# Decode attention with a gated token mixer: the last block's K halves loaded together, its neighbours' products spread, and the last projection's weights copied to 128 columns

## The chip, the cores and the metric

The kernel runs on one core of a Trainium2 chip. The metric is the device time of one execution in microseconds; times are medians over runs. Engines: PE is TensorE (PEld its weight loads), DVE is VectorE, ACT is ScalarE, POOL is GpSimd, SP is SyncE, which here issues nearly all DMAs.

## The reference

One token attends to a cache of 65536 positions; a small token mixer and a gate stand beside it.

```python
q = (x @ wq).reshape(B, Sq, Hq, Dh)            # 16 query heads, 8 KV heads, Dh = 256, D = 448
k, v = repeat(k_cache, 2), repeat(v_cache, 2)  # k_cache, v_cache: [1, 8, 65536, 256] bf16
p = softmax(einsum(q, k) * Dh ** -0.5)
a = einsum(p, v).reshape(B, Sq, Hq * Dh) @ wo
b = mixer(layernorm(x))                        # gelu(h * w1 + b1) @ w2 + b2
g = sigmoid((x * gate_w).sum(-1))
out = g * a + (1 - g) * b                      # [1, 1, 448] bf16
```

K and V together are 537 MB, read once.

## The kernel before

**Blocks.** The cache is worked in 32 blocks (`NBLK`) of 16384 positions, four (`NB`) for each KV head. Block `n` needs 8 MB of K and 8 MB of V. Partition `p` holds 128 (`VP`) consecutive positions. K of a block lies in two tiles of 4 MB, `k_tiles[0]` and `k_tiles[1]` (kn in the profile), the first and second half of each partition's positions; V lies in one tile `vt` of 8 MB. There is one buffer of each, so a load waits until the engines have read what lies there.

**Scores.** `score_block(n)` (L348) runs over 32 steps `t`. In each, `transposes` (L321) turns four 128x128 fp32 pictures of K with the identity on PE (L325) into one of the four PSUM tiles `tps`, and DVE copies it to `kT` (L330). Two and three steps after each fourth one, `scores` (L337) multiplies the transposed K by the queries into `sc_ps` (L339). Steps 0 to 15 read `k_tiles[0]`, steps 16 to 31 `k_tiles[1]`. `hooks` is a dictionary of functions that are called after given steps, so their instructions stand at that place in each engine's order.

**Softmax and products.** `softmax(n)` (L378) takes the maximum, ACT the exponential (`p_sb`, L397) and the rescaling factor `al` of the sums so far (L402); DVE transposes the probabilities into `pT` (L405). `pv(ip)` (L362) multiplies a quarter of `pT` by a quarter of `vt` into `pv_ps`: 16 matmuls of 512 columns in four column groups (L365). `pv_block` calls it four times, and `accumulate` (L413) folds `pv_ps` into `acc` (L415). After a head's fourth block, `denominators` and `head_end` project its output with `wo_sb` and add it to `a_acc`.

**Order.** The helper `seq` keeps every engine's instructions in the order in which the program names them, SP's DMA issues too. An issue that waits holds up the issues behind it. For a usual block the order on SP is V of block n, then the two K halves of block n+1.

**The last two blocks** (`L` is block 31) are written out by hand. Block 30 issues V's first half, K of block 31 first half, V's second half, K of block 31 second half:

```python
elif n == L - 1:
    load_v(n, 0, KP)
    load_k(L, 0)
    load_v(n, KP, VP)
    load_k(L, 1)
```

Block 31's V goes into the K tiles, in six pieces of 64, 32, 16, 8, 4 and 4 positions per partition (`load_v_last`, L121), as the K rows there are read. In block 31 the hook after step 17, `before_last` (L480), does all products of block 30, `accumulate`, and `project_base` (L470), which forms `base`, the sum of the other heads' gated output and the mixer, and the gate as a column `gcol`.

**The end.** The last output is built by columns. Eight base matmuls (four of fp32, each run as two, L517) put `base` into `f_ps`, which lies in `tps[0]`. Small DVE operations make `esc`, `lsv` and, behind a matmul (L527), `rdv`. `collect` (L434) starts the sums `o_ps` from `acc`; the 256 matmuls at L538 add V of block 31, two for each of the 128 positions `j`, with V as the weights and two columns of probabilities. `oT` scales them (L545), 16 matmuls (L549) multiply by the last two heads' rows of `wo_sb`, taken as 112 columns at a stride of four, and `res` (L555) goes out (L556).

Of the kernel before, what the change touches and what calls it, by code (L numbers as in the profile page):

```python
# [8 lines left out]
FP32 = mybir.dt.float32  # L9
BF16 = mybir.dt.bfloat16  # L10
ACT = mybir.ActivationFunctionType
ALU = mybir.AluOpType
AXIS = mybir.AxisListType

HQ = 16
HKV = 8
DH = 256
REP = HQ // HKV
# [10 lines left out]
def kernel(  # L29
# [48 lines left out]
    vt = kvpool.tile([128, VP, DH], BF16, name="vt")  # L78
    kT_tiles = [work.tile([128, NJ, 128, 2], BF16, name=f"kT{i}") for i in range(2)]
    p_sb = work.tile([128, 512], BF16)  # L80
    pT = work.tile([128, 512], BF16)
    wo_sb = const.tile([128, HQ, 2, D], BF16)

    tps = [psum.tile([128, 512], FP32, name=f"tps{i}") for i in range(4)]
# [221 lines left out]
    junk = work.tile([128, REP], FP32)  # L306
    nb_tiles = [work.tile([128, 1], FP32, name=f"nb{i}") for i in range(2)]
    den = work.tile([128, 1], FP32)
    al = work.tile([128, 1], FP32)
    rden = work.tile([128, 1], FP32)  # L310
    lsv = work.tile([128, REP], FP32)
    rdv = work.tile([128, REP], FP32)
    esc = work.tile([128, 2, REP], FP32)
    oT = work.tile([128, 2, REP], BF16)
    a_acc = const.tile([1, D], FP32)
    base = const.tile([1, D], FP32)
    res = const.tile([D // NCOL, NCOL], BF16)
    gcol = const.tile([128, 1], FP32)
    state = {"t": 0}

# [38 lines left out]
        while due:  # L359
            scores(n // NB, *due.pop(0)[1])  # L360

    def pv(ip):  # L362
        for jj in range(NJ):
            grp = jj % 4
            seq(nc.tensor.matmul(  # L365
                pv_ps[32 * grp:32 * grp + 2 * REP, :, :],
                lhsT=pT[:, 32 * jj + 2 * REP * ip:32 * jj + 2 * REP * (ip + 1)],
                rhs=pairs(vt[:, 32 * ip:32 * (ip + 1), :])[:, :, jj, :],
                start=(ip == 0 and jj < 4),
                stop=(ip == NI // 2 - 1 and jj >= NJ - 4),  # L370
                tile_position=(0, 32 * grp),
            ))

    def pv_block():
        for ip in range(NI // 2):
            pv(ip)

    def softmax(n):  # L378
        b = n % NB
        nb, nb_old = nb_tiles[n % 2], nb_tiles[(n + 1) % 2]  # L380
        seq(nc.vector.tensor_reduce(out=rmax[:], in_=sc_ps[:, :], op=ALU.max, axis=AXIS.X))  # L381
        seq(nc.tensor.transpose(sm_ps[0:1, 0:128], rmax[:, 0:1], ident_f[:, :]))  # L382
        seq(nc.vector.tensor_reduce(  # L383
            out=(mrun if b == 0 else mnew)[:],
            in_=sm_ps[0:1, 0:128].rearrange("o (a i r) -> o r a i", a=4, r=REP)[:, :, :, 0:NI],
            op=ALU.max, axis=AXIS.XY,
        ))
        if b > 0:
            seq(nc.vector.tensor_tensor(out=mrun[:], in0=mrun[:], in1=mnew[:], op=ALU.max))  # L389
        seq(nc.tensor.matmul(  # L390
            sm_ps[:, 128:128 + REP], lhsT=ones_f[0:1, :], rhs=mrun[0:1, :], start=True, stop=True
        ))
        seq(nc.vector.tensor_tensor_reduce(  # L393
            out=junk[:], in0=sm_ps[:, 128:128 + REP], in1=nval[:], scale=1.0, scalar=0.0,
            op0=ALU.mult, op1=ALU.add, accum_out=nb[:, 0:1],
        ))
        seq(nc.scalar.activation(  # L397
            out=p_sb[:, :], in_=sc_ps[:, :], func=ACT.Exp, scale=scale,
            bias=nb[:, 0:1], accum_out=den[:, 0:1],
        ))  # L400
        if b > 0:
            seq(nc.scalar.activation(  # L402
                out=al[:], in_=nb_old[:], func=ACT.Exp, scale=-1.0, bias=nb[:, 0:1]
            ))
        seq(nc.vector.transpose(out=pT[:, :], in_=p_sb[:, :]))  # L405
        if b > 0:
            seq(nc.vector.scalar_tensor_tensor(  # L407
                out=lsum[:], in0=lsum[:], scalar=al[:, 0:1], in1=den[:], op0=ALU.mult, op1=ALU.add
            ))
        else:  # L410
            seq(nc.vector.tensor_copy(out=lsum[:], in_=den[:]))

    def accumulate(n):  # L413
        if n % NB > 0:
            seq(nc.vector.scalar_tensor_tensor(  # L415
                out=acc[:], in0=acc[:], scalar=al[:, 0:1], in1=pv_ps[:, :, :],
                op0=ALU.mult, op1=ALU.add,
            ))
        else:
            seq(nc.vector.tensor_copy(out=acc[:], in_=pv_ps[:, :, :]))  # L420
# [10 lines left out]

    o_ps = [hd_ps[:, 464:464 + REP], sm_ps[:, 464:464 + REP]]

    def collect(weights, stop):  # L434
        for c in range(2):
            for e in range(2):
                seq(nc.tensor.matmul(  # L437
                    o_ps[c],
                    lhsT=acc[:, e, :].rearrange("p (d c) -> p c d", c=2)[:, c, :],
                    rhs=weights[:, e, :],  # L440
                    start=(e == 0), stop=(stop and e == 1),
                ))

    def project(g):
# [6 lines left out]
                ))  # L451

    def head_end(g):
        collect(esc, True)
        for c in range(2):
            seq(nc.vector.tensor_copy(out=oT[:, c, :], in_=o_ps[c]))
        project(g)
        a_ps = hd_ps[0:1, 0:D]
        if g == 0:
            seq(nc.vector.tensor_copy(out=a_acc[:], in_=a_ps))  # L460
        else:
            seq(nc.vector.tensor_tensor(out=a_acc[:], in0=a_acc[:], in1=a_ps, op=ALU.add))
# [1 line left out]
    L = NBLK - 1  # L464

    def products(n):
        pv_block()
        accumulate(n)

    def project_base():  # L470
        seq(nc.vector.scalar_tensor_tensor(
            out=base[:], in0=a_acc[:], scalar=gate[0:1, 0:1], in1=rest[:],
            op0=ALU.mult, op1=ALU.add,
        ))
        seq(nc.tensor.matmul(
            sm_ps[:, 200:201], lhsT=ones_f[0:1, :], rhs=gate[0:1, 0:1], start=True, stop=True
        ))
        seq(nc.vector.tensor_copy(out=gcol[:], in_=sm_ps[:, 200:201]))

    def before_last():  # L480
        products(L - 1)
        project_base()

    for n in range(NBLK):
        if n == 0:
            score_block(n, {8: gate_sum, 20: mixer_tail})
        elif n < L:
            score_block(n)
        else:
            score_block(n, {17: before_last})  # L490
        if n < L - 1:
            load_v(n)
            load_k(n + 1, 0)
            load_k(n + 1, 1)
            if n == 0:
                seq(nc.sync.dma_start(
                    out=wo_sb[:], in_=A_wo.rearrange("(h p c) n -> p h c n", p=128, c=2)
                ))
        elif n == L - 1:
            load_v(n, 0, KP)  # L500
            load_k(L, 0)
            load_v(n, KP, VP)
            load_k(L, 1)
        else:
            load_v_last(L)
        softmax(n)
        if n < L - 1:
            if n % NB == NB - 1:
                denominators()
            products(n)  # L510
            if n % NB == NB - 1:
                head_end(n // NB)


    f_ps = tps[0][0:D // NCOL, 0:NCOL]
    for k in range(NCOL):
        seq(nc.tensor.matmul(  # L517
            f_ps[:, k:k + 1], lhsT=base[0:1, :].rearrange("o (m k) -> o k m", k=NCOL)[:, k, :],
            rhs=ones_f[0:1, 0:1], start=(k == 0), stop=False, skip_group_check=True,
        ))  # L520
    seq(nc.vector.tensor_scalar(
        out=esc[:], in0=fst[:], scalar1=al[:, 0:1], scalar2=None, op0=ALU.mult
    ))
    seq(nc.vector.tensor_scalar(
        out=lsv[:], in0=val[:], scalar1=lsum[:, 0:1], scalar2=None, op0=ALU.mult
    ))
    seq(nc.tensor.matmul(  # L527
        hd_ps[:, 456:456 + REP], lhsT=ones_f[:, :], rhs=lsv[:, :], start=True, stop=True
    ))
    seq(nc.vector.reciprocal(out=rdv[:], in_=hd_ps[:, 456:456 + REP]))  # L530
    seq(nc.vector.tensor_scalar(
        out=rdv[:], in0=rdv[:], scalar1=gcol[:, 0:1], scalar2=None, op0=ALU.mult
    ))
    collect(esc, False)
    for j in range(VP):
        i, jj = divmod(j, NJ)
        for c in range(2):
            seq(nc.tensor.matmul(  # L538
                o_ps[c],
                lhsT=k_tiles[j // KP][:, j % KP, :].rearrange("p (d c) -> p c d", c=2)[:, c, :],  # L540
                rhs=pT[:, 32 * jj + REP * i:32 * jj + REP * (i + 1)],
                start=False, stop=(j == VP - 1),
            ))
    for c in range(2):
        seq(nc.vector.tensor_tensor(out=oT[:, c, :], in0=o_ps[c], in1=rdv[:], op=ALU.mult))  # L545
    for c in range(2):
        for r in range(REP):
            for k in range(NCOL):
                seq(nc.tensor.matmul(  # L549
                    f_ps[:, k:k + 1],  # L550
                    lhsT=wo_sb[:, HQ - REP + r, c, :].rearrange("p (m k) -> p k m", k=NCOL)[:, k, :],
                    rhs=oT[:, c, r:r + 1],
                    start=False, stop=(r == REP - 1 and c == 1), skip_group_check=True,
                ))
    seq(nc.vector.tensor_copy(out=res[:], in_=f_ps))  # L555
    seq(nc.sync.dma_start(out=out[0, 0].rearrange("(m k) -> m k", k=NCOL), in_=res[:, :]))  # L556


# [28 lines left out]
```

## Time and profile before

| | |
|---|---|
| median of 3 runs | 1296.05 us (1295.45 to 1296.85) |
| the profiled execution, its own time | 1295.6 us |
| its span, first to last instruction | 1293.7 us |
| mean granted PE clock | 0.855 |
| HBM read | 544.22 MB, 421 GB/s over the span |
| DVE copies of K, L330 | 646.5 us busy |
| PE transposes of K, L325 | 604.9 us busy |
| chain of waits that ended last | DMA 66%, PE 31%, DVE 2% |

Stretches of the profile give busy time of each engine with the number of instructions, then the granted PE clock (1.00 is full speed), the mean busy share of the 16 DMA engines and GB/s. Timeline rows are: start in us, length in us, engine, line, operation, output and inputs, count; in brackets the engine's idle time before it and what ended it. SPq rows are DMA issues, not the transfers. Times in a trace are those of one execution.

### The profile page before, as it was taken

To read this page: it belongs to the slowest core of one execution; us is meant where nothing else is said; L and a number is where in the kernel's file an instruction comes from. 1 tells how busy PE (TensorE), PEld (TensorE's weight loads), DVE (VectorE), ACT (ScalarE), POOL (GpSimd) and SP (SyncE) were. 2 spreads that over 40 slices of the span, in tenths; PEclk is the share of its full clock that TensorE was granted. 3 is DMA by queue.
4 is the path that set the end of the run, shared out by engine and by line. 5 is a ranking of instruction groups with operands and counts; after the bars stand their busy time and mean duration, and the time that the engine had idled before them with its cause. 6 is when DMAs were issued, how large, how long until landed. Compare 5 with 4: busy or idle time off the path is not lost.

```text
span 1293.7 us, 20135 instructions
## 1 busy us (share of the span) xinstructions
PE 984.2 (76%) x8761; PEld 644.0 (50%) x8761; DVE 753.0 (58%) x1360; ACT 42.8 (3%) x107; POOL 4.2 (0%) x7
## 2 busy tenths in 40 slices
PE   5767777887777787768786678876778877777857
PEld 4445444555544555445554445554445554445536
DVE  5565555665556665556764556754556655556644
ACT  4000000000000000000000000000000000000000
POOL 1000000000000000000000000000000000000000
PEclk9887878897888988888998888987888978788877
DMA  9999999999999999999999999999999999999993
GB/s 406 426 426 432 437 425 429 434 437 436 433 426 431 433 439 435 427 434 428 431 437 434 438 424 428 436 434 432 436 429 424 439 423 442 418 427 436 392 402 134
DMA packets 17838, 545.51 MB, mean 422 GB/s; under 512 B 2260, under 2 KB 4310, under 8 KB 4822
## 3 DMA queue, kind: packets, MB, share of 16 engines
q1 hardware_dynamic: 17312, 544.22, 97.9%
q8 instruction: 68, 1.11, 0.3%
q14 instruction: 20, 0.16, 0.0%
q10 hardware_dynamic: 438, 0.01, 0.0%
HBM read 544.22 MB, written 0.00 MB: 421 GB/s over the span
## 4 chain that ended last, share of the span: by engine, by line
DMA 66%; PE 31%; DVE 2%; issue 0%; ACT 0%; ACTq 0%; DVEq 0%
DMA kn<-in_A_k_cache_dram 63%; PE tps L325 23%; PE sc_ps L339 5%; DMA vt<-in_A_v_cache_dram 3%; DVE kT L330 1%; PE pv_ps L365 1%; PE sm_ps L538 0%; PE hd_ps L538 0%; PE tps L549 0%; PE hd_ps L437 0%; ACT p_sb L397 0%; DVE pT L405 0%; PE hd_ps L448 0%; DVE rmax L381 0%; PE sm_ps L437 0%
## 5 line engine op out<-in xcount | busy, mean ns | idle before, releaser
L330 DVE COPY kT<-tps 128x1024 bf16<-128x1024 bf16 x1024 | 646.5, 684 | 185.6 <-PE tps L325 184.3
L325 PE MATMUL tps<-ident_f,kn 128*128 128x128 f32 x4096 | 604.9, 297 | 110.4 <-DMA kn<-in_A_k_cache_dram 110.4
L325 PEld LDWEIGHTS tps<-ident_f,kn 128*128 128x128 f32 x4096 | 488.0, 151 | 231.1 <-issue 115.6
L365 PE MATMUL pv_ps<-vt,pT 128*4 128x512 bf16 x1984 | 176.9, 535 | 95.2 <-DMA vt<-in_A_v_cache_dram 87.7
L339 PE MATMUL sc_ps<-kT,qpad 128*32 128x512 bf16 x2048 | 201.6, 394 | 27.7 <-DVE kT L330 27.5
L365 PEld LDWEIGHTS <-pT 128*4 128x4 bf16 x1984 | 59.0, 110 | 200.4 <-issue 140.6
L415 DVE SCALAR_TENSOR_TENSOR acc<-acc,al,pv_ps 128x512 f32<-128x512 f32 x23 | 17.2, 747 | 167.6 <-PE pv_ps L365 167.6
L339 PEld LDWEIGHTS <-qpad 128*32 128x32 bf16 x2048 | 53.0, 93 | 110.3 <-issue 101.9
L397 ACT ACTIVATE p_sb<-sc_ps,nb 128x512 bf16<-128x512 f32 x32 | 22.0, 687 | 1220.3 <-DVE nb L393 1220.3
L420 DVE COPY acc<-pv_ps 128x512 f32<-128x512 f32 x8 | 5.5, 691 | 59.0 <-PE pv_ps L365 59.0
L405 DVE STREAM_TRANSPOSE pT<-p_sb 128x512 bf16<-128x512 bf16 x32 | 22.8, 711 | 28.9 <-ACT p_sb L397 28.9
L381 DVE TENSOR_REDUCE rmax<-sc_ps 128x1 f32<-128x512 f32 x32 | 22.1, 691 | 23.2 <-PE sc_ps L339 23.2
L382 PE MATMUL sm_ps<-ident_f,rmax 128*1 128x128 f32 x32 | 8.6, 270 | 25.4 <-DVE rmax L381 25.4
L390 PE MATMUL sm_ps<-mrun,ones_f 1*128 1x2 f32 x64 | 14.4, 292 | 14.1 <-DVE mrun L389 11.7
L382 PEld LDWEIGHTS sm_ps<-ident_f,rmax 128*1 128x1 f32 x32 | 2.5, 79 | 41.5 <-DVE rmax L381 41.5
L390 PEld LDWEIGHTS sm_ps<-mrun,ones_f 1*128 1x128 f32 x64 | 11.6, 225 | 20.2 <-DVE mrun L389 16.3
L393 DVE CUSTOM_DVE_ANT_0 junk<-sm_ps,nval 128x2 f32<-128x2 f32 x32 | 5.1, 159 | 17.3 <-PE sm_ps L390 17.3
L423 PE MATMUL hd_ps<-lsum,same 128*128 128x1 f32 x14 | 3.9, 348 | 13.8 <-DVE lsum L407 13.8
L423 PEld LDWEIGHTS hd_ps<-lsum,same 128*128 128x128 f32 x14 | 3.3, 294 | 14.4 <-DVE lsum L407 14.4
L437 PE MATMUL hd_ps<-esc,acc 128*128 128x2 f32 x32 | 5.5, 275 | 6.3 <-DVE acc L415 6.0
L383 DVE TENSOR_REDUCE mnew<-sm_ps 1x2 f32<-1x64 f32 x24 | 5.1, 211 | 8.7 <-PE sm_ps L382 8.7
L437 PEld LDWEIGHTS hd_ps<-esc,acc 128*128 128x128 f32 x32 | 4.8, 212 | 9.9 <-DVE acc L415 9.6
(96 smaller groups left out, 135.3 us busy)
## 6 DMA issues: line engine op xcount, KB each, us to landing
kn<-in_A_k_cache_dram SPq DMA_DIRECT2D x63, 4096.0 KB, 26.8
vt<-in_A_v_cache_dram SPq DMA_DIRECT2D x2, 4096.0 KB
kn<-in_A_k_cache_dram SPq DMA_DIRECT2D x2, 2048.0 KB, 12.4
kn<-in_A_v_cache_dram SPq DMA_DIRECT2D x1, 4096.0 KB, 17.2
wo_sb<-in_A_wo_dram SPq DMA_DIRECT2D x1, 3584.0 KB
vt<-in_A_wq_dram SPq DMA_DIRECT2D x1, 3072.0 KB, 9.9
kn<-in_A_v_cache_dram SPq DMA_DIRECT2D x1, 2048.0 KB, 7.1
kn<-in_A_v_cache_dram SPq DMA_DIRECT2D x1, 1024.0 KB, 6.8
```

Of the source, the lines that this page charges most:

```text
L325: seq(nc.tensor.transpose(tp[:, jj * 128:(jj + 1) * 128], k_tiles[i // 4][:, i % 4 * NJ + quarter * 4 + jj, :].bitcast(FP32), ident_f[:, :],))
L330: seq(nc.vector.tensor_copy(out=kT_tiles[i % 2][:, quarter * 4:(quarter + 1) * 4, :, :].rearrange("p j n c -> p (j n c)"), in_=tp[:, :].bi ...
L339: seq(nc.tensor.matmul(sc_ps[32 * a:32 * (a + 1), :], lhsT=qpad[:, c, g, i, :], rhs=kT_tiles[i % 2][:, :, 32 * a:32 * (a + 1), c], start=( ...
L365: seq(nc.tensor.matmul(pv_ps[32 * grp:32 * grp + 2 * REP, :, :], lhsT=pT[:, 32 * jj + 2 * REP * ip:32 * jj + 2 * REP * (ip + 1)], rhs=pair ...
L381: seq(nc.vector.tensor_reduce(out=rmax[:], in_=sc_ps[:, :], op=ALU.max, axis=AXIS.X))
L382: seq(nc.tensor.transpose(sm_ps[0:1, 0:128], rmax[:, 0:1], ident_f[:, :]))
L390: seq(nc.tensor.matmul(sm_ps[:, 128:128 + REP], lhsT=ones_f[0:1, :], rhs=mrun[0:1, :], start=True, stop=True))
L397: seq(nc.scalar.activation(out=p_sb[:, :], in_=sc_ps[:, :], func=ACT.Exp, scale=scale, bias=nb[:, 0:1], accum_out=den[:, 0:1],))
L405: seq(nc.vector.transpose(out=pT[:, :], in_=p_sb[:, :]))
L415: seq(nc.vector.scalar_tensor_tensor(out=acc[:], in0=acc[:], scalar=al[:, 0:1], in1=pv_ps[:, :, :], op0=ALU.mult, op1=ALU.add,))
L423: seq(nc.tensor.matmul(hd_ps[:, 460:461], lhsT=same[:].rearrange("p a r -> p (a r)"), rhs=lsum[:, 0:1], start=True, stop=True,))
L437: seq(nc.tensor.matmul(o_ps[c], lhsT=acc[:, e, :].rearrange("p (d c) -> p c d", c=2)[:, c, :], rhs=weights[:, e, :], start=(e == 0), stop= ...
```

## The change

It does five things:

1. Loads: both K halves of block 31 stand between the halves of V of block 30.
2. Products of block 30: `pv(30, 0)` and `pv(30, 1)` come after steps 8 and 14 of block 31's scores, `pv(30, 2)`, `pv(30, 3)` and `accumulate(30)` after block 31's softmax. `pT` and `al` get two buffers each for it.
3. The end is put in another order: `esc` and `lsv`, the base matmuls, the remaining products, the `lsv` matmul, `accumulate`, `rdv`. V's first 64 positions are multiplied before `collect`, which now adds to them.
4. `project_base` is split: the gate column is made in block 1, after step 5; `base` after step 4 of block 31, in a layout of four rows of 128 columns, of which 112 are used and the rest zero.
5. The last two heads' rows of `wo` are copied by ACT, after step 16 of block 1, to `wo_last`, four sets of 128 contiguous columns for each of the four row groups (112 used, the rest set to zero by POOL), and the last 16 matmuls read them.

```diff
-    pT = work.tile([128, 512], BF16)
+    pT_tiles = [work.tile([128, 512], BF16, name=f"pT{i}") for i in range(2)]
...
-    base = const.tile([1, D], FP32)
+    base = const.tile([1, NCOL, 128], FP32)
+    seq(nc.gpsimd.memset(base[:], 0.0))
+    wo_last = const.tile([128, REP, 2, NCOL, 128], BF16)
+    seq(nc.gpsimd.memset(wo_last[:], 0.0))
...
+    def result_base():
+        seq(nc.vector.scalar_tensor_tensor(
+            out=base[:, :, 0:MC], in0=a_acc[:].rearrange("o (m k) -> o k m", k=NCOL),
+            scalar=gate[0:1, 0:1], in1=rest[:].rearrange("o (m k) -> o k m", k=NCOL),
+            op0=ALU.mult, op1=ALU.add,
+        ))
+
+    def last_wo():
+        for r in range(REP):
+            for c in range(2):
+                seq(nc.scalar.copy(
+                    out=wo_last[:, r, c, :, 0:MC],
+                    in_=wo_sb[:, HQ - REP + r, c, :].rearrange("p (m k) -> p k m", k=NCOL),
+                ))
...
-            score_block(n)
+            score_block(n, {5: gate_column, 16: last_wo} if n == 1 else {})
         else:
-            score_block(n, {17: before_last})
+            score_block(n, {4: result_base, 8: lambda: pv(L - 1, 0), 14: lambda: pv(L - 1, 1)})
...
             load_v(n, 0, KP)
             load_k(L, 0)
+            load_k(L, 1)
             load_v(n, KP, VP)
-            load_k(L, 1)
...
         softmax(n)
+        if n == L:
+            ...  # esc, lsv
+            f_ps = tps[0][:, 0:NCOL]
+            for k in range(NCOL):
+                ...  # base matmuls
+            pv(n - 1, 2)
+            pv(n - 1, 3)
+            ...  # the lsv matmul
+            accumulate(n - 1)
+            ...  # rdv
...
-    collect(esc, False)
     for j in range(VP):
         i, jj = divmod(j, NJ)
         for c in range(2):
             ...
-                start=False, stop=(j == VP - 1),
+                start=(j == 0), stop=(j == VP - 1),
             ))
+        if j == KP - 1:
+            collect(esc, False, False)
...
-                    lhsT=wo_sb[:, HQ - REP + r, c, :].rearrange("p (m k) -> p k m", k=NCOL)[:, k, :],
+                    lhsT=wo_last[:, r, c, k, :],
```

More of the change, by code (lines that the diff above doesn't have):

```diff
@@ L308 @@
     den = work.tile([128, 1], FP32)
-    al = work.tile([128, 1], FP32)
+    al_tiles = [work.tile([128, 1], FP32, name=f"al{i}") for i in range(2)]
     rden = work.tile([128, 1], FP32)
@@ L315 @@
     a_acc = const.tile([1, D], FP32)
-    base = const.tile([1, D], FP32)
-    res = const.tile([D // NCOL, NCOL], BF16)
+    MC = D // NCOL
+    base = const.tile([1, NCOL, 128], FP32)
+    seq(nc.gpsimd.memset(base[:], 0.0))
+    wo_last = const.tile([128, REP, 2, NCOL, 128], BF16)
+    seq(nc.gpsimd.memset(wo_last[:], 0.0))
+    res = const.tile([MC, NCOL], BF16)
     gcol = const.tile([128, 1], FP32)
@@ L360, in score_block, with pv @@
             scores(n // NB, *due.pop(0)[1])
-    def pv(ip):
+    def pv(n, ip):
+        pT = pT_tiles[n % 2]
         for jj in range(NJ):
@@ L372, in pv @@
             ))
-    def pv_block():
-        for ip in range(NI // 2):
-            pv(ip)
     def softmax(n):
@@ L380, in softmax @@
         nb, nb_old = nb_tiles[n % 2], nb_tiles[(n + 1) % 2]
+        al, pT = al_tiles[n % 2], pT_tiles[n % 2]
         seq(nc.vector.tensor_reduce(out=rmax[:], in_=sc_ps[:, :], op=ALU.max, axis=AXIS.X))
@@ L415, in accumulate @@
             seq(nc.vector.scalar_tensor_tensor(
-                out=acc[:], in0=acc[:], scalar=al[:, 0:1], in1=pv_ps[:, :, :],
+                out=acc[:], in0=acc[:], scalar=al_tiles[n % 2][:, 0:1], in1=pv_ps[:, :, :],
                 op0=ALU.mult, op1=ALU.add,
@@ L432, with collect @@
     o_ps = [hd_ps[:, 464:464 + REP], sm_ps[:, 464:464 + REP]]
-    def collect(weights, stop):
+    def collect(weights, start, stop):
         for c in range(2):
@@ L440, in collect @@
                     rhs=weights[:, e, :],
-                    start=(e == 0), stop=(stop and e == 1),
+                    start=(start and e == 0), stop=(stop and e == 1),
                 ))
@@ L453, in head_end @@
     def head_end(g):
-        collect(esc, True)
+        collect(esc, True, True)
         for c in range(2):
@@ L466, in products, with gate_column @@
     def products(n):
-        pv_block()
+        for ip in range(NI // 2):
+            pv(n, ip)
         accumulate(n)
[L470 to L474, printed above, removed]
+    def gate_column():
         seq(nc.tensor.matmul(
@@ L478, in project_base @@
         seq(nc.vector.tensor_copy(out=gcol[:], in_=sm_ps[:, 200:201]))
-    def before_last():
-        products(L - 1)
-        project_base()
+    def result_base():
[11 more added lines that the diff above has]
+                ))
     for n in range(NBLK):
@@ L506 @@
         softmax(n)
+        if n == L:
+            seq(nc.vector.tensor_scalar(
+                out=esc[:], in0=fst[:], scalar1=al_tiles[L % 2][:, 0:1], scalar2=None, op0=ALU.mult
+            ))
+            seq(nc.vector.tensor_scalar(
+                out=lsv[:], in0=val[:], scalar1=lsum[:, 0:1], scalar2=None, op0=ALU.mult
+            ))
+            f_ps = tps[0][:, 0:NCOL]
+            for k in range(NCOL):
+                seq(nc.tensor.matmul(
+                    f_ps[:, k:k + 1], lhsT=base[0:1, k, :],
+                    rhs=ones_f[0:1, 0:1], start=(k == 0), stop=False, skip_group_check=True,
+                ))
+            pv(n - 1, 2)
+            pv(n - 1, 3)
+            seq(nc.tensor.matmul(
+                hd_ps[:, 456:456 + REP], lhsT=ones_f[:, :], rhs=lsv[:, :], start=True, stop=True
+            ))
+            accumulate(n - 1)
+            seq(nc.vector.reciprocal(out=rdv[:], in_=hd_ps[:, 456:456 + REP]))
+            seq(nc.vector.tensor_scalar(
+                out=rdv[:], in0=rdv[:], scalar1=gcol[:, 0:1], scalar2=None, op0=ALU.mult
+            ))
         if n < L - 1:
@@ L512 @@
                 head_end(n // NB)
[L515 to L533, printed above, removed]
-    collect(esc, False)
     for j in range(VP):
@@ L540 @@
                 lhsT=k_tiles[j // KP][:, j % KP, :].rearrange("p (d c) -> p c d", c=2)[:, c, :],
-                rhs=pT[:, 32 * jj + REP * i:32 * jj + REP * (i + 1)],
-                start=False, stop=(j == VP - 1),
-            ))
+                rhs=pT_tiles[L % 2][:, 32 * jj + REP * i:32 * jj + REP * (i + 1)],
+                start=(j == 0), stop=(j == VP - 1),
+            ))
+        if j == KP - 1:
+            collect(esc, False, False)
     for c in range(2):
@@ L554 @@
                 ))
-    seq(nc.vector.tensor_copy(out=res[:], in_=f_ps))
+    seq(nc.vector.tensor_copy(out=res[:], in_=f_ps[0:MC, :]))
     seq(nc.sync.dma_start(out=out[0, 0].rearrange("(m k) -> m k", k=NCOL), in_=res[:, :]))
```

## The prediction

> **What bounds the kernel now.** I read the page first (engine shares, the 40 slices), then the chain of waits in order of time, then the timeline of the last 100 us, and last the busy time by stretches of that end.
>
> ```profile
> span 1293.7 us, 20135 instructions
> PE 984.2 (76%) x8761; PEld 644.0 (50%) x8761; DVE 753.0 (58%) x1360; ACT 42.8 (3%) x107; POOL 4.2 (0%) x7
> DMA  9999999999999999999999999999999999999993
> GB/s 406 426 426 432 437 425 429 434 437 436 433 426 431 433 439 435 427 434 428 431 437 434 438 424 428 436 434 432 436 429 424 439 423 442 418 427 436 392 402 134
> ```
>
> All slices but the last have busy DMA engines at about 430 GB/s: the body waits for bytes, and the change moves the same bytes. Only the end can change, from 1240 us on, where the last slices fall to 392, 402 and 134 GB/s. The timeline there (start, length, what, idle before and its releaser):
>
> ```profile
> 1216.81 0.33 SPq L108 DMA_DIRECT2D kn<-in_A_k_cache_dram  x1
> 1217.19 0.43 SPq L114 DMA_DIRECT2D vt<-in_A_v_cache_dram  x1
> 1227.64 0.33 SPq L108 DMA_DIRECT2D kn<-in_A_k_cache_dram  x1
> ...
> 1235.27 4.64 PE L325 MATMUL tps<-ident_f,kn 128*128 128x128 f32 x24 [4.31 <-DMA kn<-in_A_k_cache_dram]
> ...
> 1254.83 1.94 PE L325 MATMUL tps<-ident_f,kn 128*128 128x128 f32 x8 [7.67 <-DMA kn<-in_A_k_cache_dram]
> ...
> 1257.11 4.80 PE L365 MATMUL pv_ps<-vt,pT 128*4 128x512 bf16 x64
> ```
>
> The three issues are K31's first half, V30's second half, K31's second half (blocks 0 to 31). PE starts block 31 at 1235.27, when the first K half lands, has transposed it by 1247.16, and then waits 7.67 us until 1254.83 for the second half, since 4 MB of V went ahead of it. Then it does 64 products of block 30 in the middle of the scores, and only after that frees the K rows that the last V pieces overwrite. The stretches show the price (length, PE, PEld, DVE, ACT, POOL busy, granted clock, DMA share, GB/s):
>
> ```profile
> 1240.00:1247.00 7.00, 7.00 (x64) 4.77 (x60) 6.53 (x11) 0.00 (x0) 0.00 (x0) 1.00 1.03 442
> 1260.50:1266.50 6.00, 5.98 (x68) 3.85 (x61) 4.39 (x8) 0.00 (x0) 0.00 (x0) 1.00 0.05 19
> 1278.50:1293.70 15.20, 10.29 (x280) 10.21 (x280) 0.46 (x4) 0.00 (x0) 0.00 (x0) 0.50 0.01 2
> ```
>
> For 6 us the DMA stands still (0.05, 19 GB/s) while half of V31 is not yet issued: its second piece goes out at 1266.55. After 1278.5 nothing is loaded; PE alone runs the end:
>
> ```profile
> 1287.28 1.73 PE L549 MATMUL tps<-oT,wo_sb 128*112 128x1 bf16 x16 [0.22 <-DVE oT L545]
> 1289.05 0.16 DVE L555 CAST res<-tps 112x4 bf16<-112x4 f32 x1 [1.75 <-PE tps L549]
> 1289.23 0.36 SPq L556 DMA_DIRECT2D out_dram<-res  x1
> ```
>
> **The change, part by part.** All sums are against the profiled execution: span 1293.7, time 1295.6, so 1.9 us lie outside the span; it is 0.45 below the median of 1296.05.
>
> *Order of loads.* K31's first half is issued as before (1216.81) and lands as before (1235.27). K31's second half still waits for PE to free its buffer, to 1227.64. Now V30's second half stands behind it on SP and goes out at about 1228.0 instead of 1217.19. The queue still has the first K half to move until 1235.27, 7.6 us after the issue, so the wait costs nothing (at worst 1 us for engines that run ahead). Halves land in the order of issue: 1235.27, 1254.7 two halves later, 1264.4 for V31's first piece (17.2 us after 1247.19), 9.7 us each. So the second K half lands at 1245.0, V30's second half at 1254.7, V31's first piece at 1264.4 as before.
> [...] The landings above came in order.
>
> *Scores of block 31.* Block 30, whose halves were both there in time, took 1205.21 to 1229.03, 23.8 us. Block 31's first half took 0.3 more (11.9 against 11.6, PE clock 0.50 at first): 24.1. Into it go: 32 of block 30's products (hooks 8 and 14), which in the timeline take 0.053 us each at clock 1.00 (36 weight loads in 1.82) and 0.107 at 0.50; the clock is 1.00 from 1240, so 1.7 us (up to 3.4); V30's first half, loaded ahead of K31, is there. `result_base` on DVE, 0.67 (its contiguous form L471; strided access is not shown, 0.5 to 1.3): PE sets the pace with 0.2 us of DVE idle in each four copies, and the products give DVE another 1.7, so 0.1 remains. Should no cover exist, 0.7. The second half, at 1248.9, no longer waits. Scores end at 1235.27 + 24.1 + 1.7 + 0.1 = 1261.2, against 1273.34.
>
> *Issue of V31.* K31's first half is free at about 1248.2 instead of 1247.19, before the 1254.7 at which the queue could start V31. The other five pieces go out from about 1255 to 1260.3, before 1264.4. So the 6 us standstill goes, and the last piece lands at 1264.4 + 9.8 = 1274.2. The stretch 1266.5 to 1278.5 moved the same 4 MB at 350 GB/s, 12 us; by that it would be 1276.4.
>
> *After the scores.* Up to pT ready: as before, 3.7 us (1273.38 to 1277.08); the 8 base matmuls end in the same time (begun 1.8 us after the scores, 1.8 long, 128 for 112 columns 2.0), so PE is free at 1261.2 + 3.8 = 1265.0. New on the path: 32 products. The granted clock fell to 0.50 at 1232.2 and 1276.5, 3.2 us after both ends of scores, so I take 0.107: 3.4 us (1.7 to 3.4), 1268.4. `lsv` matmul 0.6: 1269.0. `accumulate`, 0.75, lies beside the first 128 matmuls of V31, 0.0267 us each (256 from 1280.09 to 1286.92): 3.4, 1272.4. `collect`, 1.9 (1278.36 to 1280.23): 1274.3. The other 128, 3.4: 1277.7, each behind its piece's landing, since 1274.2 needs only the last 8. The separate `esc`, `lsv` and `rdv` instructions are those of before and hide as there. PE sets the end, 3.5 us behind the data. Before, this point was 1287.06: 9.4 saved.
> [...]
>
> *Projection.* 16 matmuls on 112 strided columns take 1.73, 0.108 each. With 128 contiguous columns the nearest row is the V product, 128 columns in bf16, 0.0267 each: 0.43 and 0.14 of drain, 0.57. 1.2 saved (0 if the columns don't matter). `res`, out DMA and close stay.
>
> *Elsewhere.* `last_wo`: four ACT copies of 448 elements, nearest row the activation of 448 at 0.75: 3.0 us in block 1, behind the landing of wo. ACT idles 33.6 us before that block's exponential at 86.82, and the products behind that wait for V until 100.40; cover 13 us. Uncovered: 3.0 once. POOL memsets: qpad took 3.52 for twice the elements, 2 us in the first 10, where PE waits for K until 16.9. `gate_column` moves from block 31 to block 1, 0.4 us of PE, under the same wait for V; in block 31 its saving is in the lines above. Two pT and al buffers cost nothing.
>
> Sum: 9.4 + 1.2 = 10.6. 1295.6 - 10.6 = **1285.0 us** (against the median 0.45 more).
>
> **The rivals.**
> *The data sets the end.* If the clock stays up or comes back, the 32 products take 1.7, `collect` 1.0 and the V matmuls less; PE then waits for the last piece: 1274.2 + 0.3 = 1274.5 instead of 1277.7, so 1281.8. For it: PE works denser after 1265 than before. Against: the 0.50 above. By only the 32 products at 0.053 it is 1283.3.
> *No earlier K half.* If K31's second half still lands at 1254.8, scores end at 1254.8 + 13.5 (18.5 less the 5.0 us of products and gate) = 1268.3; the 16.5 us behind them end at 1284.8, and the total is 1295.6 - 2.3 - 1.2 = 1292.1. Against: landings in the order of issue.
> *Slower: one lagging DMA engine.* V31's first piece had nearly all its bytes by 1260.5 but landed at 1264.4; share 0.05 is about one engine of 16. The standstill let it catch up; without, its lag rides into the last piece. It decides once that piece lands after 1277.5, and the kernel is slower by 0.2% if it lands after about 1290.6, 26 us behind the first instead of 9.8. Against: five halves at 9.7 to 10.0 us each. At 27 us behind it gives 1299.
>
> **How the numbers follow.** Forecast 0.60; data sets the end, or part of the clock, 0.25; no earlier K half 0.08; slower 0.04; a remainder without gain 0.03. All but the last two are faster by over 0.2% (2.6 us, about what a measurement of this kernel can tell from no change): 0.93, same 0.03, slower 0.04. Range: down to the data's 1281.8; up by cold products in the scores (1.7), `result_base` uncovered (0.6) and no gain in the projection (1.2), 1288.5. That leaves out the last three cases.
>
> **What would show it.** Right: no PE wait for K in the middle of block 31; no stretch without DMA between 1255 and 1273; scores ending near 1261; 32 products of block 30 behind them at 0.1 us each; V31's matmuls ending near 1277.7; a projection of 0.6 us. Wrong: a PE wait for K at half of block 31, or V matmuls broken up by waits for pieces (data sets the end), or a last piece landing after 1277.

## The result, and the profile after

The changed kernel takes 1285.82 us (median of 4 runs, 1285.52 to 1286.11) against 1295.75 (4 runs, 1295.11 to 1296.85): ratio 0.9922, interval 0.9905 to 0.9940, 9.9 us less. Forecast were 1285.0 and 10.6 less. The profiled execution took 1285.52 with a span of 1283.7, against 1295.6 and 1293.7 before: 10.1 less from trace to trace.

The page after, the lines that answer to those of before:

```profile
span 1283.7 us, 20141 instructions
PE 975.9 (76%) x8761; PEld 639.8 (50%) x8761; DVE 756.1 (59%) x1360; ACT 44.9 (3%) x111; POOL 6.3 (0%) x9
DMA  9999999999999999999999999999999999999996
GB/s 409 422 430 428 440 419 433 432 435 434 440 418 435 438 434 430 431 427 434 437 436 438 421 430 434 437 432 431 434 427 436 437 437 423 427 420 438 398 403 255
```

The body is the same; the last slice holds 255 GB/s instead of 134, because less time without loads follows the last byte. The timeline of the end (start, length, what, idle before and its releaser):

```profile
1235.25 5.38 PE L329 MATMUL tps<-ident_f,kn 128*128 128x128 f32 x24 [5.25 <-DMA kn<-in_A_k_cache_dram]
...
1242.99 1.03 PE L370 MATMUL pv_ps<-vt,pT 128*4 128x512 bf16 x16
...
1248.40 1.03 PE L370 MATMUL pv_ps<-vt,pT 128*4 128x512 bf16 x16
1249.36 1.53 PE L329 MATMUL tps<-ident_f,kn 128*128 128x128 f32 x12
...
1265.19 3.38 PE L370 MATMUL pv_ps<-vt,pT 128*4 128x512 bf16 x32
1268.50 0.38 PE L533 MATMUL hd_ps<-lsv,ones_f 128*128 128x2 f32 x2
1269.51 0.16 PE L552 MATMUL hd_ps<-pT,kn 128*128 128x2 bf16 x1 [0.63 <-DVE rdv L537]
...
1278.27 0.57 PE L565 MATMUL tps<-oT,wo_last 128*128 128x1 bf16 x16 [0.23 <-DVE oT L561]
```

PE starts at the first half's landing as before and passes into the second half (1249.36) without a wait; the 7.67 us wait of before is gone. Two quarters of block 30's products lie in the scores, two behind them. New is a wait of 0.63 us for DVE ahead of V's matmuls. The projection takes 0.57 instead of 1.73. The stretches (length, busy PE, PEld, DVE, ACT, POOL, granted clock, DMA share, GB/s):

```profile
1255.00:1260.50 5.50, 5.50 (x51) 3.92 (x50) 5.06 (x9) 0.00 (x0) 0.00 (x0) 1.00 1.09 468
1260.50:1266.50 6.00, 3.94 (x39) 2.19 (x40) 3.16 (x11) 0.96 (x3) 0.00 (x0) 0.86 0.89 380
1272.00:1278.50 6.50, 6.28 (x180) 6.21 (x178) 0.23 (x2) 0.00 (x0) 0.00 (x0) 0.50 0.04 12
```

Where the DMA stood still (19 GB/s from 1260.5 to 1266.5) it now moves 380 GB/s, and loading ends about 1274 instead of 1279.

Step by step:

| step | forecast | traced |
|---|---|---|
| K31's first half there | 1235.27 | 1235.25 |
| scores of block 31 end (last matmul) | 1261.2 | 1262.28 |
| PE begins the last 32 products | 1265.0 | 1265.19 |
| they end | 1268.4 | 1268.57 |
| V's first half begins | 1269.0 | 1269.51 |
| it ends | 1272.4 | 1272.9 |
| `collect` ends, V's second half begins | 1274.3 | 1274.5 |
| it ends | 1277.7 | 1278.05 |
| V's last piece lands | 1274.2 | 1274.3 (issued 1260.88, 13.4 to landing) |
| projection | 0.57 | 0.57 |

### The profile page after: what moved, and what is told of

It reads as the page before. It is cut to its first block, busy times and chain, and to the rows that moved or that the text cites. A ratio compares the mean times of both kernels' runs of the same rounds, so it can differ in the third digit from the quotient of the medians.

```text
span 1283.7 us, 20141 instructions
## 1 busy us (share of the span) xinstructions
PE 975.9 (76%) x8761; PEld 639.8 (50%) x8761; DVE 756.1 (59%) x1360; ACT 44.9 (3%) x111; POOL 6.3 (0%) x9
## 4 chain that ended last, share of the span: by engine, by line
DMA 68%; PE 30%; DVE 2%; issue 0%; DVEq 0%
DMA kn<-in_A_k_cache_dram 67%; PE tps L329 23%; PE sc_ps L343 5%; DVE kT L334 1%; PE pv_ps L370 0%; PE hd_ps L552 0%; PE sm_ps L552 0%; DMA xr<-in_A_x_dram 0%; PE tps L527 0%; PE hd_ps L440 0%; PE sm_ps L440 0%; DVE acc L418 0%; DVE rmax L384 0%; DVE z L278 0%; PE tps L565 0%
## 5 line engine op out<-in xcount | busy, mean ns | idle before, releaser
L370 PE MATMUL pv_ps<-vt,pT 128*4 128x512 bf16 x1984 | 172.9, 524 | 94.6 <-DMA vt<-in_A_v_cache_dram 90.8
## 6 DMA issues: line engine op xcount, KB each, us to landing
kn<-in_A_v_cache_dram SPq DMA_DIRECT2D x1, 1024.0 KB, 13.4
```

What stands on the lines that cost most here:

```text
L370: seq(nc.tensor.matmul(pv_ps[32 * grp:32 * grp + 2 * REP, :, :], lhsT=pT[:, 32 * jj + 2 * REP * ip:32 * jj + 2 * REP * (ip + 1)], rhs=pair ...
```

## The experiments

Each was run beside runs of the kernel before, whose medians were 1295.69 to 1295.88; all changes are against the changed kernel unless another is named.

**The order alone taken back.**

```diff
             load_k(L, 0)
-            load_k(L, 1)
             load_v(n, KP, VP)
+            load_k(L, 1)
```

> The changed kernel, but with the old order of the four loads (V30's second half ahead of K31's second half). Theory, the earlier K half is what pays: it lands at 1254.8 again, PE waits some 5 us for it at half of block 31, the scores end 6.0 later (1254.8 + 13.5 = 1268.3 against 1262.28), and everything behind them shifts: 1285.8 + 6.0 = 1291.8 us. Rival, the spread of block 30's products pays and the order does not matter: 1285.8.

Measured: 1292.35 us (11 runs), ratio 0.9978, interval 0.9969 to 0.9986. Timeline at half of block 31:

```profile
1254.56 1.94 PE L329 MATMUL tps<-ident_f,kn 128*128 128x128 f32 x8 [4.70 <-DMA kn<-in_A_k_cache_dram]
```

The second half lands at 1254.5 again, PE waits 4.70 for it, and the scores end at 1268.45, 6.2 later. So the place of one DMA issue is worth 6.5 of the 9.9 us by the medians. The eleven runs lie in two groups, six from 1291.61 to 1292.35 and five from 1294.19 to 1294.61; the median and the profiled run are of the lower group, in the upper one the loss is 2 to 3 us more, and what makes it stays open.

**The order alone, on the kernel before.**

```diff
             load_k(L, 0)
+            load_k(L, 1)
             load_v(n, KP, VP)
-            load_k(L, 1)
```

> The kernel before with only the new order of loads. Theory, the order needs the spread: the hook after step 17 stands at 1248.7, its first 32 products run, the other 32 wait for V30's second half until 1254.7, run at half clock until 1258.1, and the 14 steps left take 11.2 and 0.3 for the gate: scores end at 1269.7 against 1273.34, so 3.6 less than before, 1292.2 us. Rival, the order alone gives the whole gain of scores and standstill: 8.8 less, 1287.0.

Measured: 1292.70 us, ratio 0.9974, interval 0.9963 to 0.9985, and the new wait stands where it was expected:

```profile
1248.08 1.90 PE L365 MATMUL pv_ps<-vt,pT 128*4 128x512 bf16 x32
1254.50 3.58 PE L365 MATMUL pv_ps<-vt,pT 128*4 128x512 bf16 x32 [4.52 <-DMA vt<-in_A_v_cache_dram]
```

The load that went back in the order is now the late one: the second 32 products wait 4.52 for V. The order alone gives 3.2 us (this run), everything but the order 3.5 (the run above, with the projection's 1.2 in it); together they give 9.9. They are one change: whoever moves a load forward has to move the use of the one behind it back.

**The projection on 112 columns.**

```diff
-                    f_ps[:, k:k + 1],
-                    lhsT=wo_last[:, r, c, k, :],
+                    f_ps[0:MC, k:k + 1],
+                    lhsT=wo_sb[:, HQ - REP + r, c, :].rearrange("p (m k) -> p k m", k=NCOL)[:, k, :],
```

> The changed kernel with the last 16 matmuls (and the base ones, for the same 112 rows) on 112 columns, the 16 from wo_sb at stride four. wo_last is still made. Theory: 0.108 instead of 0.027 us each, 1.2 more: 1287.0 us. Rival, the columns do not matter: 1285.8.

The base matmuls are on 112 columns here too, for the same 112 rows. Measured: 1287.0 us (1286.58 to 1287.11), 1.2 more, and the 16 matmuls take what they took before:

```profile
1277.91 1.73 PE L565 MATMUL tps<-oT,wo_sb 128*112 128x1 bf16 x16 [0.23 <-DVE oT L561]
```

The run doesn't part 128 columns from contiguous ones. V's matmuls, 128 columns at stride two and 0.0267 us each, speak for the 128; no run here has 128 columns at stride four.

**All 64 products behind the softmax.**

```diff
-            score_block(n, {4: result_base, 8: lambda: pv(L - 1, 0), 14: lambda: pv(L - 1, 1)})
+            score_block(n, {4: result_base})
...
-            pv(n - 1, 2)
-            pv(n - 1, 3)
+            for ip in range(NI // 2):
+                pv(n - 1, ip)
```

> The changed kernel with all 64 products of block 30 behind block 31's softmax. Theory, a product's price goes by the clock of its place (0.053 us in the scores, 0.107 behind them): scores end 1.9 earlier, the 64 products take 5.8 to 6.8 instead of 3.4 for 32: 0.5 to 1.5 more, 1286.3 to 1287.3 us. Rival, the place does not matter, a product costs the same in both: 1285.6 to 1285.9.

Measured: 1285.82 us (1284.43 to 1286.24), no difference in the medians: the time of the rival, but not by its reason. The timeline, and two stretches behind it, first of this kernel, then of the changed one:

```profile
1263.93 5.73 PE L370 MATMUL pv_ps<-vt,pT 128*4 128x512 bf16 x64
```
```profile
1268.50:1273.50 5.00, 4.38 (x142) 3.50 (x135) 1.05 (x3) 0.00 (x0) 0.00 (x0) 1.00 0.47 186
1273.50:1276.00 2.50, 2.50 (x74) 2.50 (x71) 0.00 (x0) 0.00 (x0) 0.00 (x0) 0.81 0.03 7
```
```profile
1268.50:1273.50 5.00, 4.37 (x138) 4.30 (x134) 1.06 (x3) 0.00 (x0) 0.00 (x0) 0.82 0.65 258
1273.50:1276.00 2.50, 2.50 (x63) 2.50 (x63) 0.00 (x0) 0.00 (x0) 0.00 (x0) 0.50 0.04 11
```

The scores end 2.1 earlier (1260.16), the products cost 2.35 more. The base matmuls, at half clock here, take 1.84 instead of 1.17, so the products end 1.1 later (1269.66 to 1268.57): behind the scores they cost more, as the theory had it. In both kernels the clock is back at 1268.24, but here it falls only at 1275.07, there at 1271.65: `collect` takes 1.1 instead of 1.85, and V's second half ends at 1278.28, 0.2 later than in the changed kernel. Most of what the place costs, the clock gave back in this trace.

**Two mends for the new wait of 0.63.** The reciprocal ahead of `accumulate` on DVE; or the `lsv` sum in a PSUM tile of its own.

```diff
-            accumulate(n - 1)
             seq(nc.vector.reciprocal(out=rdv[:], in_=hd_ps[:, 456:456 + REP]))
+            accumulate(n - 1)
```


> The changed kernel with the reciprocal (rdv) ahead of accumulate(30) on DVE. Theory, V's first matmul waits for the reciprocal, which reads the PSUM tile that it writes, and the reciprocal stands behind accumulate's 0.75: 0.6 less, 1285.2 us, and V's matmuls begin 0.25 to 0.3 behind the lsv matmul instead of 0.63. Rival, accumulate was beside the matmuls as the prediction had it, and the wait is another's: 1285.8.


```diff
-                hd_ps[:, 456:456 + REP], lhsT=ones_f[:, :], rhs=lsv[:, :], start=True, stop=True
+                tps[1][:, 0:REP], lhsT=ones_f[:, :], rhs=lsv[:, :], start=True, stop=True
...
-            seq(nc.vector.reciprocal(out=rdv[:], in_=hd_ps[:, 456:456 + REP]))
+            seq(nc.vector.reciprocal(out=rdv[:], in_=tps[1][:, 0:REP]))
```


> The changed kernel with the lsv sum in tps[1], a PSUM tile of its own, instead of in the tile of V's sums; the order on DVE stays. Theory, the wait of 0.63 ahead of V's matmuls is for that shared tile and goes altogether: 1285.2 us. Rival, it is accumulate itself that PE waits for: 1285.8.

Measured: 1286.09 (1285.28 to 1286.64) and 1285.02 (1284.53 to 1285.73). V's first matmul, first mend and second:

```profile
1269.94 0.16 PE L552 MATMUL hd_ps<-pT,kn 128*128 128x2 bf16 x1 [0.26 <-DVE rdv L536]
```
```profile
1268.55 0.17 PE L552 MATMUL hd_ps<-pT,kn 128*128 128x2 bf16 x1
```

The wait is 0.26 with the first and gone with the second, though `accumulate` still stands ahead of the reciprocal there. So the wait is for the reader of the shared tile, as the theory said. The times only half bear it out: the first mend shows no gain. A wait of 0.4 is less than these runs differ among themselves, and in the second one's trace the clock came back early (below).

**`result_base` out of block 31.**

```diff
-            score_block(n, {5: gate_column, 16: last_wo} if n == 1 else {})
+            score_block(n, {1: {5: gate_column, 16: last_wo}, L - 2: {5: result_base}}.get(n, {}))
         else:
-            score_block(n, {4: result_base, 8: lambda: pv(L - 1, 0), 14: lambda: pv(L - 1, 1)})
+            score_block(n, {8: lambda: pv(L - 1, 0), 14: lambda: pv(L - 1, 1)})
```

> The changed kernel with result_base in block 29, after step 5, instead of in block 31 after step 4. Theory, its 1.0 us on DVE stand in the way of the copies there, with no products ahead to give cover: scores end 0.7 earlier and so does the kernel, 1285.1 us. Rival, the products after steps 8 and 14 give it back, as the prediction had it (0.1): 1285.7.

Measured: 1285.94 us (1285.51 to 1286.88): nothing, the rival's answer. In its trace the scores did end earlier, 26.1 us behind K's landing instead of 27.1, but the traces laid side by side show that this is the clock. From K31's landing to the return of the full clock, and to the first reduction behind the scores:

| kernel | clock back after | scores done after |
|---|---|---|
| changed | 5.7 | 27.08 |
| changed, run again | 5.5 | 26.95 |
| reciprocal first | 4.8 | 26.70 |
| own PSUM tile | 3.0 | 25.78 |
| `result_base` early | 3.7 | 26.13 |

The first four hold `result_base` and lie near a line of 0.47 us for each us of half clock; on it, 3.7 gives 26.1. The fifth, without `result_base`, lies at 26.13. My theory of a 0.7 us cost was the clock, read as DVE.

**The clock held up.** 16 matmuls of 512 columns in PE's wait for K; their result is overwritten.

```diff
         softmax(n)
+        if n == L - 1:
+            for _ in range(16):
+                seq(nc.tensor.matmul(
+                    tps[3][:, :], lhsT=ident[:, :],
+                    rhs=wo_last[:, 0, 0, :, :].rearrange("p k m -> p (k m)"), start=True, stop=True
+                ))
```

> The changed kernel with 16 more matmuls of 512 columns behind block 30's softmax, whose result is overwritten: about 3.5 us of PE work in its wait for K. Theory, the time from K's landing to the end of the scores goes by when the clock comes back (2.9 to 5.7 us after the landing in the runs so far, 0.47 us of scores for each of them): with no drop it is 24.4 instead of 25.8 to 27.1, and the kernel takes 1283.5 us, 1.5 to 2.5 less than the changed kernel beside it. Rival, the scores go by the copies on DVE and not by the clock: 1285.8.

The changed kernel ran beside it:

> The changed kernel itself, as the measure for the other three on the same chip: 1285.8 us, and between runs up to 1.3 apart, if the end of the scores goes by the clock's chance (0.47 us for each of up to 2.8).

Measured: 1283.99 us (1282.40 to 1287.67) against 1285.29 (1285.11 to 1285.82). Stretches after K's landing, first of the changed kernel, then of this one:

```profile
1235.00:1238.00 3.00, 2.89 (x14) 2.89 (x15) 1.42 (x3) 0.00 (x0) 0.00 (x0) 0.50 0.99 426
1238.00:1241.00 3.00, 3.00 (x18) 2.38 (x17) 2.68 (x4) 0.00 (x0) 0.00 (x0) 0.57 1.01 437
```
```profile
1235.00:1238.00 3.00, 2.75 (x24) 2.60 (x24) 2.05 (x4) 0.00 (x0) 0.00 (x0) 1.00 0.99 426
1238.00:1241.00 3.00, 2.60 (x29) 1.61 (x32) 3.00 (x5) 0.00 (x0) 0.00 (x0) 1.00 1.04 448
```

The clock does not fall before 1267.4, and the scores end 24.8 us behind the landing instead of 26.95: the mechanism is shown. In this trace the 32 products also run at full clock (1.90 us instead of 3.33), which the theory had not counted. The time follows by 1.3 in the median with a spread of 5, so the size of the gain is not settled. Part of it goes in a new stop:

```profile
1271.17 0.17 PE L558 MATMUL sm_ps<-pT,kn 128*128 128x2 bf16 x1
1272.02 0.18 PE L558 MATMUL hd_ps<-pT,kn 128*128 128x2 bf16 x1 [0.68 <-issue]
```

PE stops in the middle of V's second half and goes on at 1272.02. It does not wait for V: the 151st of the 256 matmuls stands there, position 75 (counted from 0), and its piece (32 positions, issued at 1253.23, 15.8 us to landing) lay there from 1269.1. The profile names nothing that released it (`issue`). The stop returns in the kernel with all mends below, 16 matmuls later without the 16 extra ones (first two rows) and at the same matmul with them (last two):

```profile
1272.83 0.17 PE L551 MATMUL sm_ps<-pT,kn 128*128 128x2 bf16 x1
1273.07 0.19 PE L551 MATMUL hd_ps<-pT,kn 128*128 128x2 bf16 x1
...
1272.26 0.17 PE L557 MATMUL sm_ps<-pT,kn 128*128 128x2 bf16 x1
1272.53 0.18 PE L557 MATMUL hd_ps<-pT,kn 128*128 128x2 bf16 x1
```

So it goes by the place in PE's program. Its cause is not shown; no run changes that alone.

**All mends together.** `result_base` early, the sum in its own tile, and a third quarter of block 30's products after step 26 of the scores (`26: lambda: pv(L - 1, 2)`, so that only `pv(n - 1, 3)` is left behind the softmax); run twice, and once more with the 16 matmuls.

> Both of the last two together, and a third quarter of block 30's products in the scores (after step 26), so that one quarter is left behind the softmax. Theory: scores end at 1262.28 - 0.7 + 0.9 = 1262.5; the last quarter runs 3.0 to 4.7 behind that, the lsv matmul to 1267.6, V's first half to 1271.0, collect to 1272.9, V's second half to 1276.3 instead of 1278.06: 1.8 less, 1284.0 us. Rival, the data sets the end once PE is earlier (V's second half waits for its pieces, the last lands about 1274): at least 1276.0 all the same, but with waits in the matmuls; or the late third quarter costs more than it saves: 1285 to 1286.

> The version with both mends and three quarters in the scores once more, beside the changed kernel: 1.8 less than it, if the sum of its parts holds; 0 to 0.5 less if its earlier time came from the chance of the clock.

> The same 16 matmuls in the version with both mends and three quarters in the scores. Theory, from here the data sets the end: scores end 1.3 to 2 earlier, but the last piece of V lands at 1274.0 to 1274.4, so V's second half waits for its pieces and ends at 1274.5 instead of 1275.6: 1282.8 us. Rival, PE still sets the end: 1281.9 or less.

Measured: 1283.85 (ratio to before 0.9909, interval 0.9896 to 0.9923), the second time 1284.44 (0.9912, 0.9899 to 0.9926; 0.85 less than the changed kernel beside it, not 1.8), and 1283.99 with the 16 matmuls. The medians are 0.9 to 2.0 us below the changed kernel's, but the ranges of the runs overlap and so do the intervals. The theory that the data then sets the end fails: with the 16 matmuls V's second half ends at 1275.5, and the only stop in it (0.27 us at 1272.26) is the one shown above. In that trace they bring the end of the scores 1.0 closer to the landing (25.7 us instead of 26.65), but the clock falls at 1262.97 instead of 1265.67, and the base matmuls (1.65 to 1.03) and the last 16 products (1.88 to 1.12) take 1.4 more. That the first median met the 1284.0 expected was in part luck: the sum counted the 0.7 of `result_base` that the run above does not bear out. In the second trace without them, with the clock back after 5.3 us as beside the changed kernel (5.5), V's second half ends only 0.45 earlier (1277.33 to 1277.78). A step to about 1284 is likely and not proved.

## Why the prediction was right, point by point

- **The order of the loads** did what the sum said: the second half is there when PE gets to it (1249.36), where the kernel before waited for it until 1254.83, and the standstill of the DMA goes too. The first and second experiments show that this step needs both its parts. The rival "no earlier K half" fell at once; its time, 1292.1, is what the old order gives (1292.35), since it describes that very kernel.
- **The end of the scores** came 1.1 later than forecast. The mis-sized term is the start of the block: I took 0.3 us for the half clock, from a trace in which the clock came back 3.7 us after the landing. Here it came after 5.7, 0.9 more by the 0.47 above. The 32 products in the scores took some 2.0 (27.08 less the 25.13 of the kernel without them, clock back after 5.7 and 5.85) instead of 1.7. `result_base` was rightly put at next to nothing, though it took 1.02 on DVE.
- **Behind the scores** two errors met: PE was done with the base matmuls 2.9 us behind the scores instead of 3.8 (they took 1.17 us instead of 2.0, most of it at full clock), and `accumulate` was not beside V's matmuls. The step that failed reads "lies beside the first 128 matmuls of V31": V's sums share a PSUM tile with the `lsv` sum, and the reciprocal that reads it stands behind `accumulate`. I had called the order of `rdv` that of before; the 0.26 wait of before grew to 0.63.
- **32 products at half clock, 3.4 us:** 3.38, with some luck. The reason given, a fall of the clock 3.2 us after the end of the scores, is no fixed delay: it fell 2.55 after it here, 0.36 ahead of the products, and 1.1 to 3.6 after it in the other traces but one; with the clock held up the products took 1.90.
- **V's matmuls:** as forecast. The first rival supposed that they gain by the full clock. They hardly do: the first half ran at 1.00 until 1271.65 at 0.025 us each, the second at 0.50 at 0.0267. What a full clock does shorten is the scores (24.8 instead of 26.95), the products (1.90 instead of 3.33) and `collect` (1.1 instead of 1.85). Even so the data set the end in no trace: with the clock held up V's second half ends at 1275.0, and the last piece had landed at 1274.0, ahead of its matmuls.
- **The slower rival,** one lagging DMA engine: the lag is there (a share of 0.06 and 25 GB/s from 1273 to 1274, one engine of 16) and rides into the last piece, but it doesn't grow. The last piece lands at 1274.3, and PE, which begins V's second half at 1274.5, needs it only for the last 8 matmuls.
- **Projection:** 1.2 forecast, 1.2 by the third experiment. **`last_wo`:** 2.12 us on ACT at 81.21, ahead of the exponential at 87.11, no cost.

Sum: forecast 10.6, measured 10.1 between the profiled executions (9.9 between the medians). By the table the 0.5 is the scores (+1.1), the base matmuls (-0.9), the gap ahead of V's matmuls (+0.3), `collect` (-0.3) and V's second half (+0.2), so 0.35 at its end, and 0.2 behind it. The forecast is close in part because the first two errors nearly cancel.

## What to carry to other kernels

At the end of this stream the order of the last loads was worth more than any other part of the change (6.5 of the 9.9 us by the first experiment), but only with the consumers put in the same order: name for each load what is queued behind its first use. A forecast of the end can be added up row by row if each row is taken with its clock; then expect an error of about 1 us from where the steps of the clock happen to lie (the scores of the four kernels with `result_base` in block 31 ended 25.78 to 27.08 us behind the landing), and do not read a difference of that size between two traces as the effect of an edit before the clock's rows have been laid side by side. A PSUM tile shared by a short sum and a long one tied the long one to whoever read the short one (0.63 us here, nothing with a tile of its own).

## What the runs showed of the hardware that was not expected

- The granted clock came back 2.9 to 5.9 us after the same PE work began, from run to run. This is less chance than it looks: in each trace that shows several steps of the clock they lie on one grid of 3.41 us (in the kernel before 1232.18, 1239.01, 1249.25, 1259.49, 1276.55: apart by 2, 3, 3 and 5 of them; in the changed kernel 1230.69, 1240.93, 1264.83, 1268.24, 1271.65: by 3, 7, 1 and 1), and what differs is where PE's work falls on it. The clock came back at the end of an interval of the grid in which PE had started 0.53 us late (all mends, 1234.96 to 1238.37, PE from 1235.49), not of one with 1.14 (changed, 1234.11 to 1237.52, PE from 1235.25). The spread seen here, 3.0 us, is less than one interval.
- With two columns a matmul costs 0.025 us at full and 0.0267 at half clock: there the clock is nearly free. With 512 columns it is 0.053 and 0.107.
- Products of 512 columns brought the clock back where they filled 3.0 us of such an interval (changed, to 1268.24), not where they filled 2.2 of it and the narrow base matmuls the rest (reciprocal first, to 1267.74). 7 us of unbroken matmuls of two columns did not (kernel before, from 1280.09, granted 0.50 to the end), and during them it falls (at 1271.65 in the changed kernel, at 1275.07 with all 64 behind the softmax).
- PE lost 0.2 to 0.8 us at one place of its own program in three traces (with the 16 matmuls, with all mends, with both). In the second trace of all mends, where V's matmuls began 2.0 us later (1268.66 to 1266.7), it lost nothing there. What released PE is not shown.
